# Late stage of an attention and GLU kernel: raw tokens in tiles of their own, output weights in the early ones' place, and a plan in which two DMA queues share one rate

## The chip, the cores and the metric

The kernel runs on one core of a Trainium2 chip. A core has five engines that run side by side, each through its own instruction list in order: TensorE (PE in the profile; PEld are its weight loads), VectorE (DVE), ScalarE (ACT), GpSimd (POOL) and SyncE (SP). SP and POOL also issue the transfers between the chip's memory (DRAM) and the core's SBUF; each has a queue of its own, and sixteen DMA engines move the data of both. TensorE writes to PSUM banks, from which VectorE and ScalarE read. The metric is the device time of one execution in microseconds, as the median of several runs; less is better.

## The reference

Attention over 32 heads (batch 4, heads 8, 768 tokens, 64 values each), in which a query sees only the keys whose six sign bits, taken from a projection, equal its own; then, on the joined heads (3072 tokens of 512 values), a gated layer with 1536 inner channels.

```python
q_bits = (np.einsum('bhsd,dk->bhsk', q, proj) > 0).astype(np.int64)    # keys alike
mask = q_bucket[:, :, :, None] == k_bucket[:, :, None, :]
scores = np.where(mask, scale * np.matmul(q, k.transpose(0, 1, 3, 2)), -1e9)
attn = softmax(scores)                                     # with 1e-9 added to the sum
x = np.matmul(attn, v).transpose(0, 2, 1, 3).reshape(B * S, H * D)
gate = 1.0 / (1.0 + np.exp(-(x @ w_gate)))
return (gate * (x @ w_val) @ w_out).astype(np.float32)
```

The weights of the layer arrive as 64-bit floats, which the kernel turns into 32-bit ones from their two integer halves.

## The kernel before

**A plan in the program.** The kernel doesn't emit its instructions in the order of its source. Each step is a task for one engine (or a choice of two) with a key, a duration in ns, the tasks it comes after, and the buffers (counted by name in `stock`, and in `late_stock` from the switch on) that it takes and gives. `Plan.order` (line 84) runs through time with these durations: each engine, when free, starts the ready task with the lowest key, and at the same key the one that was added first. The order that comes out is that of the instructions of each engine, and on the chip each engine then keeps it, whatever the real times are. A transfer (`dma`, line 312) takes its queue 600 ns and has a tail until its data count as landed: 2000 ns plus its bytes at 240 bytes per ns, behind the earlier transfers of the same queue. `wire` keeps this for the SP and the POOL queue apart, as if each had the whole rate (lines 156 to 161).

**Two stages.** Attention fills the first half of the span; its results go to DRAM as tokens `xd`. Beside it an early part of the gated layer runs (`moe_early`): for each batch and half, the first two blocks of 128 inner channels (J1 = 2), whose sums go to DRAM as `part`, by way of `ob` buffers of which there are two. Meanwhile the other weights are converted, combined and kept in DRAM, up to block 10. At `switch` (line 1206) the buffers of attention are given back and the late stage begins; the last early units still run into it.

**The late stage** (`products`, line 630) goes through the batches one by one. Each does its 768 tokens as two halves of 384 and the remaining inner channels in ten visits: jp from 1 to 5, and for each the gate and the value weights, streamed from DRAM by POOL's queue. A visit computes a 2 x 2 block product with seven products instead of eight (Strassen's scheme in Winograd's form). So it needs seven operands of the tokens: four blocks as they are and combinations of them. Before, they are made so: x0 = B11, x1 = B21, x3 = B22, x4 = B12 - B11, x5 = B22 - x4, x2 = B22 - B12, x6 = B21 - x5. Each is split into a high half, rounded (ScalarE, line 669), and a low half, the rest (VectorE, line 672); differences are VectorE's (line 664). In a visit the operands are used in the order x0, x1, x5, x4, x2, x6, x3 (the products m1, m2, m6, m5, m7, m4, m3, line 784), six matmuls each, and after the second, the fifth and the seventh TensorE does a piece of an output product (`y`, line 570). ScalarE copies interim sums to `t` tiles (t1, t16, t167, line 792), VectorE adds them to the other bank (line 799). From a gate visit come sigmoids (`sig`, line 856), in a value visit VectorE multiplies (lines 870 and 872) and the product is split into high and low again (lines 877 and 880).

**Tiles of the tokens.** x0, x2 and x3 use the tiles of the early part (`xr`, `xh`, `xl`), the other operands their own. The raw blocks B11 and B21 are loaded into the low halves of x0 and x1 themselves (line 652), which the low step then overwrites; B12 and B22 go into a tile `xb` (line 657). So the load of the next batch's B11 waits for the last visit's first product of this batch, and that of B21 for the second. Differences go to three tiles xt0 to xt2, that of x2 over B12.

**Late weights.** Blocks 10 and 11 (jp = 5) are loaded and converted in the first batch's visits (`load_w`, `load_pair`): first two output weights, then four chunks of gate and value weights, by way of one raw buffer. Steps of the conversion stand on lines 338 to 361, splits on 408, 411, 470 and 473, the store to DRAM on 476. Output weights 2 to 9 come back from DRAM (line 419).

**Ends of a batch.** The six pieces of the last output products run in the first visits of the next batch. Each is then added (`whole`, line 729) to the early part's sum, fetched from `part` into an `ob` buffer (line 743), and stored (line 746); fetches are chained one behind the other. The last batch uses the free token tiles instead.

Of the kernel before, what the change touches and what calls it, by code (L numbers as in the profile page):

```python
# [43 lines left out]
class Task:  # L44
# [7 lines left out]
    def __init__(self, key, options, after, take, give, tail, kind, behind=()):  # L52
# [11 lines left out]
        self.ready, self.size = 0, 0  # L64


class Plan:
# [16 lines left out]
    def order(self):  # L84
# [24 lines left out]
        while events:  # L109
# [10 lines left out]
            while again:  # L120
                again = False
                for e in SEEN:
# [60 lines left out]
def lsh_attention_glu_kernel(ctx, tc, q, k, v, proj, w_gate, w_val, w_out, out):  # L183
# [107 lines left out]
    def busy():  # L291
# [5 lines left out]
        ef=4, raw1=1, mid1=1, raw2=1, mid2=1, wk=1, xr=1, x=1, ob=2,  # L297
        t=0, zt=0, ws0=0, ws1=0, ws2=0, xb=0, xt0=0, xt1=0, xt2=0, x1=0, x4=0, x5=0, x6=0, wk2=0,
# [13 lines left out]
    def dma(key, nbytes, emit, engine="sp", **kw):  # L312
        t = add(key, engine, 600, emit, tail=LANDING + int(nbytes / RATE), **kw)
        t.size = nbytes
        return t
# [7 lines left out]
    def floats(key, load, after, last, name):  # L323
# [39 lines left out]
        a = dma(key, 524288, load_, after=after, take=[place])  # L363
# [11 lines left out]
    slots = dict(n=0, last=None)  # L375

    def load_w(key, n, j, early, last=None):
# [19 lines left out]
        def high():  # L397
            if early or last:
                if n == "o":
                    z["w"] = (later["w"] if last else w1).tile([P, 2, N_EL], F32R, name=f"w{n}{j}", tag=f"w{n}{j}")  # L400
# [15 lines left out]
        def fetch():  # L416
            w = later["w"].tile([P, 2, N_EL], F32R, name=f"w{n}{j}", tag=f"w{n}{j}")
# [3 lines left out]
        h = add(key, "act", 560, high, after=[e], take=[] if early or last else ["wk"])  # L421
# [73 lines left out]
    def load_x(u, b, g, stored):  # L495
# [19 lines left out]
        for c in range(KC):  # L515
            prev = add(
                FIRST, "act", 415, lambda c=c: high(c), after=[a, prev], take=["x"] if c == 0 else []
# [9 lines left out]
    def product(key, u, n, j, x, prev, last, pace=None):  # L527
# [14 lines left out]
        for c in range(KC):  # L542
            prev = add(
                key if c == 0 else OPEN, "pe", 3 * MM, lambda c=c: part(c), after=[prev, x["ready"][c], made[n, j], pace],
                take=z["bank"] if c == 0 else [], give=(["x"] + (["ws0"] if last == "end" else [])) if last and c == KC - 1 else [],
# [84 lines left out]
    def products(key, pair, prev, ends):  # L630
# [10 lines left out]
        TAG = dict(x0="xr", x2="xh", x3="xl")  # L641

        def slot(n):
            tag = TAG.get(n)
            X[n] = (xp if tag else later["w"]).tile(HALF_X, F32R, name=f"{n}_{b}", tag=tag or n)
            return f(X[n])

        raw = lambda n: f(X[n])[:, 1]

        def load_half(n, h):  # L650
            slot(n)
            nc.sync.dma_start(raw(n), xd_(h, 0))

        def load_second():
            X["b"] = later["w"].tile([P, 2, 2, GN], F32, name=f"xb_{b}", tag="xb")
            for h in range(2):
                nc.sync.dma_start(X["b"][:, h], xd_(h, 1))

        def difference(n, tag, first, second):
            if tag:  # L660
                X["r" + n] = later["w"].tile([P, 2, GN], F32, name=f"r{n}_{b}", tag=tag)
            else:
                X["r" + n] = X["b"][:, 0]
            nc.vector.tensor_sub(X["r" + n], first(), second())

        def high(n, of):
            if n not in X:
                slot(n)
            nc.scalar.copy(X[n][:, 0], of())

        def low(n, of, eng):
            eng.tensor_sub(X[n][:, 1], of(), f(X[n])[:, 0])

        here = lambda n: (lambda: raw(n))
        diff = lambda n: (lambda: X["r" + n])
        b12, b22 = (lambda: X["b"][:, 0]), (lambda: X["b"][:, 1])

        def lows(n, of, after, give=()):
            return add(
                FIRST, "dve", 900, lambda: low(n, of, nc.vector), after=after, give=give,  # L680
            )

        was = [a for g in range(NG) for a in stored[b, g]] + in_turn["x"]
# [580 lines left out]
```

## Time and profile before

| | |
|---|---|
| median of 3 runs | 1084.75 us (1080.46 to 1087.05) |
| profiled execution, its own time | 1079.3 us |
| its span, first to last instruction | 1077.5 us |
| mean granted clock of TensorE | 0.988 |
| TensorE busy, 553 to 600 us | 42.38 of 47.00 us |
| TensorE busy, 600 to 697 us | 91.10 of 97.00 us |
| TensorE busy, 697 to 818 us (one batch) | 117.09 of 121.00 us |
| TensorE busy, 818 to 937 us (one batch) | 115.46 of 119.00 us |
| TensorE busy, 937 us to the end | 129.79 of 140.50 us |

The profile is of one execution; its times run from the first instruction. The span is shorter than that execution's own time by 1.8 us, which lie before its first and after its last instruction. An engine's busy time counts its instructions; a wait is the idle time in front of one, put down to what ended last. The granted clock is the share of full speed that TensorE was given. "to landing" is the time from the issue of a transfer to its last data.

### The profile page before, as it was taken

What the parts mean: (1) busy time and instruction counts of PE and PEld (TensorE: products, weight loads), DVE (VectorE), ACT (ScalarE), POOL (GpSimd) and SP (SyncE); (2) the same over time, 40 slices, a digit from 0 to 9 for tenths busy, and PEclk for the clock granted to TensorE, in tenths of its full rate; (3) what the DMA queues carried; (4) which work ended last, traced back from release to release, by engine and by line L of the source; (5) the groups of instructions that cost most, each with busy time, mean ns of one, the idle gap of its engine ahead of it and who ended that gap; (6) DMA issues with size and microseconds to landing.
All of it is one profiled execution on the core that took longest, in us unless ns stands there. A gap on an engine that the chain in (4) does not pass through costs nothing.

```text
span 1077.5 us, 20497 instructions
## 1 busy us (share of the span) xinstructions
PE 1024.9 (95%) x8169; PEld 811.4 (75%) x8172; DVE 697.8 (65%) x1464; ACT 567.1 (53%) x1011; POOL 202.8 (19%) x230
## 2 busy tenths in 40 slices
PE   9999898999999999989999899999998999979998
PEld 5665566676675766656677789889997999879997
DVE  6898978889989778987746673464236333444333
ACT  2777776777786776857635433333234232422331
POOL 0013235344442423422031000000000000000000
PEclk9999998999999999999999999999999999989999
DMA  8345364764766456553168796466435743565521
GB/s 205 84 133 154 113 199 134 252 189 153 231 192 198 155 179 195 191 170 113 39 230 290 272 328 242 166 231 228 166 137 214 260 180 137 180 220 196 189 85 59
DMA packets 114561, 196.38 MB, mean 182 GB/s; under 512 B 61217, under 2 KB 83745, under 8 KB 109345
## 3 DMA queue, kind: packets, MB, share of 16 engines
q1 hardware_dynamic: 108544, 121.66, 36.0%
q0 software_dynamic: 5760, 73.40, 18.5%
q8 instruction: 64, 1.05, 0.4%
q14 instruction: 33, 0.26, 0.1%
q10 hardware_dynamic: 160, 0.00, 0.0%
HBM read 140.51 MB, written 41.94 MB: 169 GB/s over the span
## 4 chain that ended last, share of the span: by engine, by line
PE 77%; DVE 12%; DMA 6%; ACT 3%; issue 2%; POOL 1%; SPq 0%; ACTq 0%; DVEq 0%; POOLq 0%
PE y L570 13%; PE pv L1117 10%; PE sc L1034 8%; PE zBg L784 7%; PE zBv L784 7%; PE tp L1100 5%; PE zDg L784 4%; DVE e L1048 3%; PE zDv L784 3%; PE zo L570 3%; PE zg L537 3%; PE zv L537 3%; PE sc L1039 2%; PE zAg L784 2%; DMA x<-xd 2%
## 5 line engine op out<-in xcount | busy, mean ns | idle before, releaser
L1067 ACT ACTIVATE e<-e,st 128x768 f32<-128x768 f32 x192 | 196.5, 1026 | 71.6 <-DVE st L1060 71.5
L1048 DVE TENSOR_SCALAR_CACHE_REDUCE e<-sc 128x768 f32<-128x768 f32 x192 | 178.0, 951 | 21.8 <-PE sc L1039 21.2
L570 PE MATMUL y<-wo,gh 128*128 128x512 f32 x480 | 152.2, 399 | 0.0
L1117 PE MATMUL pv<-ef,vr 128*64 128x384 f32 x768 | 142.0, 499 | 0.0
L1100 PEld LDWEIGHTS tp<-ident,e 64*128 64x128 f32 x2304 | 85.5, 140 | 36.0 <-issue 20.2
L784 PE MATMUL zBv<-x,wsv 128*128 128x384 f32 x480 | 98.6, 340 | 9.9 <-ACT t167v L792 5.8
L570 PEld LDWEIGHTS y<-wo,gh 128*128 128x128 f32 x480 | 91.1, 190 | 15.7
L1100 PE MATMUL tp<-ident,e 64*128 64x64 f32 x2304 | 97.2, 227 | 5.3 <-ACT ef L1107 1.8
L784 PE MATMUL zBg<-x,wsg 128*128 128x384 f32 x480 | 97.3, 337 | 5.1 <-ACT t167g L792 3.7
L784 PEld LDWEIGHTS zBv<-x,wsv 128*128 128x128 f32 x480 | 86.5, 191 | 17.1 <-ACT t167v L792 7.4
L1107 ACT COPY ef<-tp 128x768 f32<-128x768 f32 x107 | 83.4, 792 | 25.5 <-PE tp L1100 25.2
L1034 PE MATMUL sc<-kh,ql 64*128 64x384 f32 x192 | 86.0, 448 | 9.2 <-DVE e L1048 2.9
L570 PE MATMUL y<-wo,gl 128*128 128x512 f32 x240 | 94.4, 393 | 0.0
L784 PEld LDWEIGHTS zBg<-x,wsg 128*128 128x128 f32 x480 | 85.7, 189 | 11.2 <-ACT t167g L792 4.4
L877 ACT CAST gh<-zt 128x384 fp32r<-128x384 f32 x80 | 41.0, 514 | 100.9 <-DVE zt L872 83.4
L1034 PE MATMUL sc<-kh,qsl 64*128 64x384 f32 x192 | 86.0, 448 | 7.1 <-DVE ef L1107 3.8
L1107 DVE COPY ef<-tp 128x768 f32<-128x768 f32 x85 | 80.4, 950 | 18.7 <-PE tp L1100 18.5
L1117 PEld LDWEIGHTS pv<-ef,vr 128*64 128x64 f32 x768 | 48.4, 137 | 52.5 <-issue 48.0
L1127 POOL TENSOR_TENSOR xs<-xs,rb 128x384 f32<-128x384 f32 x32 | 34.5, 1079 | 182.5 <-DVE xs L1124 117.6
L1039 PE MATMUL sc<-kb,qb 64*128 64x384 bf16 x384 | 65.2, 335 | 0.0
L1034 PE MATMUL sc<-kh,qsh 64*128 64x384 f32 x192 | 64.4, 335 | 0.0
L1034 PE MATMUL sc<-kl,qh 64*128 64x384 f32 x192 | 64.3, 335 | 0.0
(194 smaller groups left out, 2092.5 us busy)
## 6 DMA issues: line engine op xcount, KB each, us to landing
wsg<-kzg POOLq DMA_DIRECT2D x20, 1792.0 KB, 7.7
wsv<-kzv POOLq DMA_DIRECT2D x20, 1792.0 KB, 8.2
kzg<-wkg SPq DMA_DIRECT2D x10, 896.0 KB
kzv<-wkv SPq DMA_DIRECT2D x10, 896.0 KB
kr<-in_k_dram SPq DMA_DIRECT2D x64, 96.0 KB
qr<-in_q_dram SPq DMA_DIRECT2D x32, 192.0 KB
vr<-in_v_dram SPq DMA_DIRECT2D x16, 384.0 KB
qsh<-qh SPq DMA_DIRECT2D x32, 192.0 KB
```

What stands on the lines that cost most here:

```text
L537: nc.tensor.matmul(z["acc"][:, :GN], a[:, wc], x[xx][:, c, :], start=(c == 0 and i == 0), stop=(c == KC - 1 and i == 2),)
L570: nc.tensor.matmul(acc, a[:, slot, ts_], w, start=(first and i == 0), stop=(last and i == 2))
L784: nc.tensor.matmul(acc, streams[n, jp][:, c, wa, a_], X[x_][:, xa, c], start=first and c == 0 and i == 0, stop=c == 1 and i == 2, skip_gro ...
L877: nc.scalar.copy(side["h"][:, blk], w["z", blk])
L1034: nc.tensor.matmul(sc[:, j, :GN], q_[rows, c], z["k" + x][rows, h * GN : (h + 1) * GN], start=(m == 0), stop=False, tile_position=(j * D, 0),)
L1039: nc.tensor.matmul(sc[:, j, :GN], z["qb"][rows, c], z["kb"][rows, h], start=False, stop=True, tile_position=(j * D, 0),)
L1048: nc.vector.tensor_scalar(sp(e), gz["sc", t, h][:, :, :GN], -SCALE, None, op0=ALU.mult, op1=ALU.min, accum_out=gz["st", t][:, 0, h : h + 1],)
L1067: nc.scalar.activation(e, e, AF.Exp, bias=st[:, 2, h : h + 1], scale=st[:, 1, h : h + 1], accum_out=gz["su"][:, h * GT + t : h * GT + t + 1],)
L1100: nc.tensor.transpose(tp[:, r, at_ : at_ + D], gz["e", t, h][rows, c * P : (c + 1) * P], ident[rows, rows], tile_position=(r * D, 0),)
L1107: copy(gz["ef", c].rearrange("p (n r d) -> p r n d", r=2, d=D), gz["tp", c][:, :, :GN].rearrange("p r (n d) -> p r n d", d=D),)
L1117: nc.tensor.matmul(gz["pv"][rows, :GN], z["v"][:, h, c], gz["ef", c][:, h * GN : (h + 1) * GN], start=(c == 0), stop=(c == NC - 1), tile_p ...
L1127: nc.gpsimd.tensor_mul(gz["xs"], gz["xs"], gz["rb"])
```

## The change

- **Raw tokens.** B11 and B21 are loaded into tiles r0 and r1 of their own (in place of xt0 and xt1; r2 in place of xt2). The load no longer waits for the operands of the batch before, only for r0, r1 and xb. The combinations are formed in another order: T3 = B22 - B12 (over B12), T2 = T3 + B11 (in r2), T1 = B22 - T2 (over B11, after the low of x0), T4 = B21 - T2 (over B21, after the low of x1); x4 = T1, x5 = T2, x2 = T3, x6 = T4. Each operand is prepared when its own tile is given back, and these come back one by one: x2 and x3 are counted apart, and x2 is given after m7.
- **Late output weights** 10 and 11 take the tiles of the early ones 0 and 1 (`home`), after the last early products; they are loaded behind the gate and value weights instead of ahead of them.
- **Buffers.** Three `ob` instead of two, three `t` instead of two, two raw buffers for late weights instead of one.
- **The plan.** Two queues share the rate: where one has work on its wire, the other's transfer takes longer, and lengthens that. Loads of late weights and fetches of output sums count as landed 3000 ns later (`slack`). Token steps count 930 and 830 ns, where it was 900 and 800.

```diff
                     if t.tail:
                         free[e] = max(now, self.landings[0]) + ns
-                        self.wire[e] = max(self.wire[e], free[e]) + t.size / RATE
-                        t.tail = max(t.tail, self.wire[e] + LANDING - free[e])
+                        other = "sp" if e == "pool" else "pool"
+                        begin, alone = max(self.wire[e], free[e]), t.size / RATE
+                        both = max(0, self.wire[other] - begin)
+                        takes = alone + min(alone, both / 2)
+                        self.wire[e] = begin + takes
+                        self.wire[other] += min(both, takes) / 2
+                        t.tail = max(t.tail, self.wire[e] + LANDING + t.slack - free[e])
...
-        ef=4, raw1=1, mid1=1, raw2=1, mid2=1, wk=1, xr=1, x=1, ob=2,
+        ef=4, raw1=1, mid1=1, raw2=2, mid2=1, wk=1, xr=1, x2=1, x3=1, ob=3,
...
-    late_stock = dict(wk2=1, y=6, t=2, zt=3, xt0=1, xt1=1, xt2=1, ws1=1, ws2=1, xb=1, x1=1, x4=1, x5=1, x6=1)
+    late_stock = dict(wk2=1, y=6, t=3, zt=3, r0=1, r1=1, r2=1, ws1=1, ws2=1, xb=1, x1=1, x4=1, x5=1, x6=1)
...
-        a = dma(key, 524288, load_, after=after, take=[place])
+        a = dma(key, 524288, load_, slack=3000 if last else 0, after=after, take=[place])
...
+    def home(j):
+
+        early = j if j < J1 else j - NJ + J1 if j >= NJ - J1 else None
+        pool, tag = (later["w"], f"wo{j}") if early is None else (w1, f"wo{early}")
+        return pool.tile([P, 2, N_EL], F32R, name=f"wo{j}", tag=tag)
...
-        h = add(key, "act", 560, high, after=[e], take=[] if early or last else ["wk"])
+        h = add(key, "act", 560, high, after=[e] + (g_free if last else []), take=[] if early or last else ["wk"])
...
-        was = [a for g in range(NG) for a in stored[b, g]] + in_turn["x"]
-        l0 = dma(FIRST, 393216, lambda: load_half("x0", 0), after=was, take=["xr"])
+        was = [a for g in range(NG) for a in stored[b, g]]
+        l0 = dma(FIRST, 393216, lambda: load_first("B11", 0), after=was, take=["r0"])
         lb = dma(FIRST, 786432, load_second, after=was, take=["xb"])
-        l1 = dma(FIRST, 393216, lambda: load_half("x1", 1), after=was, take=["x1"])
+        l1 = dma(FIRST, 393216, lambda: load_first("B21", 1), after=was, take=["r1"])
...
+        def operand(n, of, after, give=()):
+            h = add(FIRST, "act", 830, lambda: high(n, of), after=after, take=["xr" if n == "x0" else n])
+            ready[n] = dve(lambda: low(n, of), [h], give=give)
...
-        h0 = highs("x0", here("x0"), [l0])
-        t1 = differences("x4", "xt0", b12, here("x0"), [l0, lb])
-        ready["x0"] = lows("x0", here("x0"), [h0, t1])
-        t2 = differences("x5", "xt1", b22, diff("x4"), [t1])
-        h4 = highs("x4", diff("x4"), [t1], ["x4"])
-        ready["x4"] = lows("x4", diff("x4"), [h4, t2], ["xt0"])
-        t4 = differences("x6", "xt2", here("x1"), diff("x5"), [t2, l1])
-        h1 = highs("x1", here("x1"), [l1])
-        ready["x1"] = lows("x1", here("x1"), [h1, t4])
...
+        d3 = dve(t3, [lb])
+        d2 = dve(t2, [d3, l0], take=["r2"])
+        operand("x0", "B11", [l0])
+        operand("x1", "B21", [l1])
+        operand("x5", "T2", [d2])
+        d1 = dve(t1, [d2, ready["x0"]])
+        operand("x4", "T1", [d1], ["r0"])
+        operand("x2", "T3", [d3])
+        d4 = dve(t4, [ready["x1"], d2], give=[])
+        operand("x6", "T4", [d4], ["r1"])
+        operand("x3", "B22", [lb])
+        add(FIRST, "sp", 0, lambda: None, after=[ready["x5"], d1, d4], give=["r2"])
+        add(FIRST, "sp", 0, lambda: None, after=[ready["x2"], ready["x3"], d1, d2], give=["xb"])
...
-                        FIRST, 262144, lambda: fetch(u, t, z), after=[parts[b, u, t]] + in_turn["ob"] + (list(ready.values()) if m is not None else []), take=take,
+                        FIRST, 262144, lambda: fetch(u, t, z), slack=3000, after=[parts[b, u, t]] + in_turn["ob"] + (list(ready.values()) if m is not None else []), take=take,
...
                     for late in range(JP2, JPN):
-                        for j in (2 * late, 2 * late + 1):
-                            load_w(1e3, "o", j, False, m1)
                         for w_ in "gv":
                             for c in range(2):
                                 load_pair(1e3, w_, late, c, m1)
+                        for j in (2 * late, 2 * late + 1):
+                            load_w(1e3, "o", j, False, m1)
...
-            prev = m7 = m(prev, "B", S3, "x2", False, False, [e16])
+            prev = m7 = m(prev, "B", S3, "x2", False, False, [e16], give=used("x2"))
...
-            prev = m3 = m(prev, "D", S4, "x3", False, True, [c22, *held], give=[slot_[1]] + used("x"))
+            prev = m3 = m(prev, "D", S4, "x3", False, True, [c22, *held], give=[slot_[1]] + used("x3"))
```

More of the change, by code (lines that the diff above doesn't have):

```diff
@@ L63, in __init__ @@
                 self.waits += 1
-        self.ready, self.size = 0, 0
+        self.ready, self.size, self.slack = 0, 0, 0
 class Plan:
@@ L310, in lsh_attention_glu_kernel, with dma @@
     CROWDED = 1600000
-    def dma(key, nbytes, emit, engine="sp", **kw):
+    def dma(key, nbytes, emit, engine="sp", slack=0, **kw):
         t = add(key, engine, 600, emit, tail=LANDING + int(nbytes / RATE), **kw)
-        t.size = nbytes
+        t.size, t.slack = nbytes, slack
         return t
@@ L399, in high @@
                 if n == "o":
-                    z["w"] = (later["w"] if last else w1).tile([P, 2, N_EL], F32R, name=f"w{n}{j}", tag=f"w{n}{j}")
+                    z["w"] = home(j)
                 else:
@@ L516, in load_x @@
             prev = add(
-                FIRST, "act", 415, lambda c=c: high(c), after=[a, prev], take=["x"] if c == 0 else []
+                FIRST, "act", 415, lambda c=c: high(c), after=[a, prev], take=["x2", "x3"] if c == 0 else []
             )
@@ L544, in product @@
                 key if c == 0 else OPEN, "pe", 3 * MM, lambda c=c: part(c), after=[prev, x["ready"][c], made[n, j], pace],
-                take=z["bank"] if c == 0 else [], give=(["x"] + (["ws0"] if last == "end" else [])) if last and c == KC - 1 else [],
+                take=z["bank"] if c == 0 else [], give=(["x2", "x3"] + (["ws0"] if last == "end" else [])) if last and c == KC - 1 else [],
             )
@@ L641, in products, with raw @@
         TAG = dict(x0="xr", x2="xh", x3="xl")
[L643 to L651, printed above, removed]
+        RAW = dict(B11="r0", B21="r1", T2="r2")
+        R = {}
+        def raw(n):
+            R[n] = later["w"].tile([P, 2, GN], F32, name=f"{n}_{b}", tag=RAW[n])
+            return R[n]
@@ L652, in load_half, with load_first @@
+        def load_first(n, h):
             nc.sync.dma_start(raw(n), xd_(h, 0))
         def load_second():
-            X["b"] = later["w"].tile([P, 2, 2, GN], F32, name=f"xb_{b}", tag="xb")
+            both = later["w"].tile([P, 2, 2, GN], F32, name=f"xb_{b}", tag="xb")
+            R["B12"], R["B22"] = both[:, 0], both[:, 1]
             for h in range(2):
[L657 to L664, printed above, removed]
@@ L666, in high @@
-        def high(n, of):
[L667 to L681, printed above, removed]
@@ L683, in products, with low @@
-        was = [a for g in range(NG) for a in stored[b, g]] + in_turn["x"]
-        l0 = dma(FIRST, 393216, lambda: load_half("x0", 0), after=was, take=["xr"])
+                nc.sync.dma_start(both[:, h], xd_(h, 1))
+        def high(n, of):
+            X[n] = (xp if n in TAG else later["w"]).tile(HALF_X, F32R, name=f"{n}_{b}", tag=TAG.get(n, n))
+            nc.scalar.copy(X[n][:, 0], R[of])
+        def low(n, of):
+            nc.vector.tensor_sub(X[n][:, 1], R[of], f(X[n])[:, 0])
+        was = [a for g in range(NG) for a in stored[b, g]]
@@ L685, in products @@
+        l0 = dma(FIRST, 393216, lambda: load_first("B11", 0), after=was, take=["r0"])
         lb = dma(FIRST, 786432, load_second, after=was, take=["xb"])
-        l1 = dma(FIRST, 393216, lambda: load_half("x1", 1), after=was, take=["x1"])
+        l1 = dma(FIRST, 393216, lambda: load_first("B21", 1), after=was, take=["r1"])
         ready = {}
-        def highs(n, of, after, take=()):
-            return add(FIRST, "act", 800, lambda: high(n, of), after=after, take=list(take))
-        def differences(n, tag, first, second, after):
-            return add(FIRST, "dve", 900, lambda: difference(n, tag, first, second), after=after, take=[tag] if tag else [])
```

33 lines of the change are left out of this document (18 added, 15 removed).

## The prediction

> **What bounds the kernel now.** I read the page first, then the waits of TensorE in the late stage, then granted clocks by window, then the timeline around each wait, then the chain of waits between them. The page (engine, busy us, share, instructions):
>
> ```profile
> span 1077.5 us, 20497 instructions
> ...
> PE 1024.9 (95%) x8169; PEld 811.4 (75%) x8172; DVE 697.8 (65%) x1464; ACT 567.1 (53%) x1011; POOL 202.8 (19%) x230
> ```
>
> TensorE is busy 95% of the span. The change leaves its instructions and, in the late stage, nearly all of their order as they are, since every product there is chained to the one before. So only TensorE's idle time there, and clock lost behind it, can go. The waits of TensorE from 580 us on (total us, times, longest):
>
> ```profile
> PE zAg L784 <- DVE x L672: 6.3, 3, 2.1
> PE zBv L784 <- ACT t167v L792: 5.8, 4, 1.9
> PE zBv L784 <- ACT t16v L792: 4.2, 1, 4.2
> PE zBg L784 <- ACT t167g L792: 3.7, 2, 3.0
> PE zBg L784 <- DVE zt L870: 1.4, 1, 1.4
> ```
>
> The first two rows are the three changes of batch (but for one wait in row two, below), the third is one wait near 960 us, the last two lie near 612 and 630 us. Windows (us; PE, PEld, DVE, ACT, POOL busy; granted clock; DMA share; GB/s) show that there is nothing between them (79.99 of 80 us busy) and that some waits also cost clock:
>
> ```profile
> 704.28:708.20 3.92, 3.92 (x12) 3.47 (x13) 3.88 (x5) 1.99 (x3) 0.00 (x0) 0.56 0.45 190
> ...
> 825.21:827.57 2.36, 2.36 (x11) 2.11 (x12) 2.36 (x3) 0.65 (x1) 0.00 (x0) 1.00 0.77 323
> ...
> 720.00:800.00 80.00, 79.99 (x420) 74.18 (x419) 29.88 (x56) 24.50 (x50) 3.69 (x7) 1.00 0.52 190
> ```
>
> **Part A: raw tokens in own tiles, summed ahead.** The first change of batch, in the timeline (start, us, engine, line, what; idle before and its releaser in brackets):
>
> ```profile
> 688.63 1.41 SPq L652 DMA_DIRECT2D x<-xd  x2
> 694.82 0.84 ACT L669 CAST x<-x 128x768 fp32r<-128x768 f32 x1 [2.23 <-DMA x<-xd]
> 694.82 0.96 DVE L664 TENSOR_TENSOR rx<-xb,x 128x768 f32<-128x768 f32 x1 [2.78 <-DMA x<-xd]
> 696.60 0.47 ACT L792 COPY t167v<-zBv 128x384 f32<-128x384 f32 x1
> 697.12 1.33 PE L784 MATMUL zBv<-x,wsv 128*128 128x384 f32 x6 [1.58 <-ACT t167v L792]
> 701.93 0.95 DVE L664 TENSOR_TENSOR rx<-x,rx 128x768 f32<-128x768 f32 x1
> 704.28 1.88 PE L784 MATMUL zAg<-x,wsg 128*128 128x384 f32 x5 [2.12 <-DVE x L672]
> ```
>
> The raw half of x0 can be loaded only when the last visit's first product has freed its tile (688.63). It lands at 694.8; ScalarE stands in order behind it with a token copy at its head, the copy t167v comes late, TensorE waits 1.58 us; then VectorE still has the differences before the low half of x1, and TensorE waits 2.12. Both name the load's landing as the start. After the change the four raw loads of a batch, 1.57 MB as before (first row below: size of one; second row: a weight stream and its us to landing),
>
> ```profile
> x<-xd SPq DMA_DIRECT2D x8, 384.0 KB
> ...
> wsg<-kzg POOLq DMA_DIRECT2D x20, 1792.0 KB, 7.7
> ```
>
> wait for r0, r1 and xb, which come free when the previous preparation ends, a whole batch earlier; T3 and T2 are made there and then, and the first order of business at the change is x0, then x1, in the order of use. The count stays: 4 differences and 7 lows on VectorE, 7 highs on ScalarE. What goes: 6.3 + 5.8 less the one wait of row two that is no change of batch,
>
> ```profile
> 598.39 1.32 PE L784 MATMUL zBv<-x,wsv 128*128 128x384 f32 x6 [0.62 <-ACT t167v L792]
> ```
>
> = 11.5 us, and the lost clock of the first change: the same stretch (five matmuls of zAg, two pieces of y and up to the next zBg) took 3.92 us there at 0.56 of the clock and 2.36 at the second change: 1.56. Together 13.0.
>
> The Trainium skill, "TensorE: Matmul & The Clock Gate", Part 1, says that the clock halves only after an idle window of about 3.4 us, which runs free of the kernel. The trace has a gap of 2.12 us with the clock lost and, at 825.21, one as long without. By that rule the 1.56 hangs on no gap of this length and may stay: the forecast would be 1065.4 where it is 1063.8 below.
>
> What comes in its place is VectorE's load. Back to back its steps take, and TensorE's groups take (chain of waits, start, us):
>
> ```profile
> 702.02 0.87 DVE rx L664
> 702.89 0.47 DVE gl L880
> ...
> 709.42 1.04 PE zDg L784 x6
> ...
> 711.50 1.39 PE y L570 x6
> ```
>
> A visit is 7 x 1.04 + 3 x 1.39 = 11.45 us. From the end of the last visit's second group (2.08) to the next visit's fifth, which needs the bank that the first sum frees (11.45 + 3 x 1.04 + 1.39 = 15.96), there are 13.9 us. In them VectorE has 3 sums, 4 gates and 4 lows of the gate at 0.47 (5.2), nine token steps at 0.87 (7.8), one more sum (0.47) and one output sum (0.7): 14.2, so 0.3 too much, and token steps of the new batch stand ahead of its sums, since they are numbered first at the same key. If the last two (1.74) and the output sum are ahead of it the wait is 2.4 us; if not, 0. I take 0.8 a change, nearer to the 0.3 of the count: 2.4. A third t tile loosens ScalarE's copies; I cost it at nothing. Part A: -10.6, between -13.0 and -5.8.
>
> **Part B: third output buffer and 3 us more in the plan for output fetches.** The wait near 960 us:
>
> ```profile
> 952.85 3.29 SPq L743 DMA_DIRECT2D ob_2l<-part  x2
> 954.03 0.53 POOL L1217 DMA_DIRECT2D wsv<-kzv  x1 [13.32 <-PE zDg L784]
> ...
> 962.71 0.69 DVE L729 TENSOR_TENSOR ob_2l<-y,ob_2l 128x512 f32<-128x512 f32 x1 [4.83 <-DMA ob_2l<-part]
> ...
> 964.84 2.29 PE L784 MATMUL zBv<-x,wsv 128*128 128x384 f32 x6 [4.15 <-ACT t16v L792]
> ...
> 971.06 1.23 PE L784 MATMUL zDv<-x,wsv 128*128 128x384 f32 x6
> ```
>
> The second 256 KB fetch leaves SP by 956.1 at the latest and lands at 962.7, 6.6 us on, beside a weight stream from the other queue. The plan reckoned 0.6 to issue, 2 and 262144/240 = 1.1 us, so it put the output sum 3 us too early in VectorE's order, and a gate, a high and t16v were caught behind it. With 3 us of slack, and up to 1.1 more for the shared rate, the sum is placed about where the data arrive; three fetches rather than two are ahead. What goes: 4.15, and clock: from 964.84 to 971.06 there are 6.22 us for groups of 1.04 + 1.39 + 1.04 = 3.47, so 2.75. Together 6.9. What is late next: the raw loads of the following batch now share SP's queue with these fetches at the first two changes. Between 0 (landing covered by the slack) and 6.9 (one such wait); I take 1.0, nearer the lower end because two buffers showed one such wait in three batches. Part B: -5.9.
>
> **Part C: late weights (two raw buffers, slack, shared rate, output weights last and in the early ones' tiles).** The first visits:
>
> ```profile
> 601.51 0.38 SPq L453 DMA_DIRECT2D rawg<-in_moe_w_gate_dram  x1
> ...
> 610.20 0.43 DVE L338 TENSOR_SCALAR exg<-rawg 128x512 int32<-128x512 int32 x1 [4.70 <-DMA rawg<-in_moe_w_gate_dram]
> ...
> 611.80 1.94 PE L784 MATMUL zBg<-x,wsg 128*128 128x384 f32 x6 [3.03 <-ACT t167g L792]
> ...
> 616.93 1.23 PE L784 MATMUL zBv<-x,wsv 128*128 128x384 f32 x6
> ...
> 617.28 0.32 SPq L476 DMA_DIRECT2D kzg<-wkg  x1
> ...
> 627.40 0.94 ACT L470 CAST wkg<-mfg 128x896 fp32r<-128x896 f32 x1 [3.11 <-DMA kzg<-wkg]
> ...
> 629.99 1.31 PE L784 MATMUL zBg<-x,wsg 128*128 128x384 f32 x6 [1.41 <-DVE zt L870]
> ```
>
> The raw load took 8.7 us where the plan had 2 + 2.2; now it has 7.2, and up to 2.2 more while POOL's queue moves. The store, by the landing times of this tile,
>
> ```profile
> DMA to landing us min/median/max: 8.3/9.0/9.7
> ```
>
> took 8.3 to 9.7 to free its buffer where the plan had 5.8, now up to 9.6. Two raw buffers let the next load run under the conversion. What goes: 3.03; its clock, 611.80 to 616.93 for 1.04 + 1.04 + 1.39, 1.66; and 1.41: 6.1. The conversions keep their count, so their steps still push the copies about: between 0 and all 6.1 stays; I take a quarter, 1.6, since every landing that TensorE waited for is now covered in the plan. Loading gate and value weights first has them in memory sooner; the output weights are needed only at the end of the first batch, some 100 us on, and their new tiles are free once the last early products are done, so I cost both at nothing; without that cover the first visits would gain a wait like the 3.03. Part C: -4.5.
>
> **Part D: the head of the late stage.** The first batch's raw loads no longer wait for the last early unit's tokens:
>
> ```profile
> 553.27 0.37 SPq L501 DMA_DIRECT2D xr<-xd  x1
> ...
> 562.49 0.44 PE L537 MATMUL zg<-xh,we 128*128 128x384 f32 x1 [0.65 <-ACT xh L508]
> ```
>
> They may let TensorE fill small waits such as this one, or run ahead of xr. The window
>
> ```profile
> 553.00:600.00 47.00, 42.38 (x216) 37.24 (x215) 25.16 (x35) 23.36 (x42) 9.07 (x10) 1.00 0.86 314
> ```
>
> has 47.00 - 42.38 = 4.6 us without TensorE and moves 314 GB/s, so 1.57 MB ahead of xr would be 5.0 us. Between -4.6 and +5.0; I take 0, since the early units come first at the same key.
>
> **Sum.** -10.6 - 5.9 - 4.5 + 0 = -21.0. The profiled execution took 1079.3 us (span 1077.5 and 1.8 around it): 1058.3. It lay 5.45 under the median of the three runs (1084.75), so on the median's footing 1063.8, said as 1064.
>
> **Rivals.** (1) VectorE takes back the changes of batch: the waits move from zAg to the group that needs the first sum's bank. For it: the 14.2 against 13.9; against: the token steps now have a whole visit before. Price 2.4 instead of 0.8 at three changes and the 1.56 of clock: +6.4, 1070. (2) DMA still lands later than planned, B and C stay: for it, DMA engines 0.86 busy from 553 to 600; against, the slack matches the measured 6.6 and 8.7. 1084.75 - 10.6 = 1074. (3) Slower: the raw loads stand in SP's queue ahead of transfers that TensorE will need sooner. Each such wait costs up to 6.9 with its clock (part B); three (head, first and second change) only eat the gain, and from five on, two at each change and one at the head, 34.5 - 21.0 = 13.5 makes 1098. For it: 1.57 MB is now issued next to the output fetches, beside a stream of 1.8 MB. Against: fetches of the previous batch are numbered before it. The Trainium skill, "DMA: Bandwidth & Descriptors", Issuing engines are not separate DMA queues, says that transfers of all queues interleave on the same 16 engines, so a load brought forward delays others; the 8.7 and 6.6 us above agree. (4) Nothing to see: the waits were caught elsewhere, 1080 to 1085.
>
> **How the numbers follow.** Forecast 0.56, rival one 0.18, two 0.14, three 0.07, four 0.05. A difference under about 1% (10.8 us) cannot be told from none here. Faster by more than that means below 1073.9: the forecast, all of one but a little (0.17) and less than half of two (0.05): 0.78. Slower is rival three, 0.07. The rest, 0.15, is within 1%. The range reaches down to all 26.0 gone with runs close to the profile (1053.3), and up over rival two: 1054 to 1076. The likeliest case alone spans 1056 to 1070.
>
> **What would show it.** Right: no SP wait for x0's tile before the raw loads; at a change of batch zBv and zAg wait under 1 us, and the granted clock stays 1.00 from 700 us on; output sums and conversions do not wait for DMA over 2 us. Wrong: a wait of zDg or zBg for a VectorE sum with token lows just ahead of it (rival one); a VectorE wait for ob or raw tiles with t16 or t167 behind it (rivals two and three); TensorE waits of over 3 us between 553 and 600. The whole falls if TensorE's late idle time stays above 20 us.

## The result, and the profile after

| | before | after |
|---|---|---|
| median | 1082.61 us (1078.39 to 1087.05, 4 runs) | 1053.32 us (1051.00 to 1056.21, 4 runs) |
| ratio of the times | | 0.973, 95% interval 0.968 to 0.978 |
| profiled execution | 1079.3 us | 1056.21 us, the longest of the four |
| span, mean clock | 1077.5 us, 0.988 | 1054.4 us, 0.995 |

The kernel is faster by 29.3 us at the median and by 23.1 between the two profiled executions. The forecast was 1064, with a range from 1054 to 1076: the direction was right and the gain too small, so that the time lies 0.7 below the range. The page of the changed kernel begins:

```profile
span 1054.4 us, 20508 instructions
...
PE 1017.8 (97%) x8172; PEld 807.4 (77%) x8172; DVE 699.9 (66%) x1464; ACT 566.2 (54%) x1011; POOL 203.6 (19%) x230
```

The operations of TensorE are the same; its busy time fell by 7.1 us, about what the lower clock had cost (0.988 and 0.995 of the two spans). The waits of TensorE from 555 us on (total us, times, longest; zg, zv and zo are products of the early units, zA, zB and zD the banks of the late visits):

```profile
PE zo L581 <- ACT sig L600: 2.0, 1, 2.0
PE zBv L789 <- ACT t167v L797: 0.9, 1, 0.9
PE zo L581 <- POOL gl L569: 0.9, 1, 0.9
PE zg L548 <- ACT xh L519: 0.6, 1, 0.6
PE zg L548 <- POOL xl L522: 0.6, 1, 0.6
PE zBg L789 <- ACT t167g L797: 0.6, 1, 0.6
PE zg L548 <- DVE xl L522: 0.4, 1, 0.4
```

All of them but the second lie before 600 us. From there on TensorE is busy without a break; the window's columns are us, then busy time of PE, PEld, DVE, ACT, POOL, the granted clock, DMA share and GB/s:

```profile
600.00:1040.00 440.00, 439.05 (x2300) 408.39 (x2299) 205.41 (x371) 157.29 (x302) 19.01 (x36) 1.00 0.57 208
```

Before, from 600 us to where the tail begins:

```profile
600.00:1063.00 463.00, 442.91 (x2275) 408.72 (x2274) 200.91 (x361) 155.44 (x297) 18.99 (x36) 0.99 0.54 195
```

The first change of batch in the timeline of the changed kernel, where before there were waits of 1.58 and 2.12:

```profile
688.30 1.57 ACT L671 CAST x<-B 128x768 fp32r<-128x768 f32 x2
689.45 0.95 DVE L674 TENSOR_TENSOR x<-B,x 128x768 fp32r<-128x768 f32 x1
...
696.21 4.91 SPq L661 DMA_DIRECT2D B<-xd  x2
...
699.15 1.20 PE L789 MATMUL zAg<-x,wsg 128*128 128x384 f32 x6
...
701.07 0.96 DVE L674 TENSOR_TENSOR x<-xb,x 128x768 fp32r<-128x768 f32 x1
701.58 1.21 PE L789 MATMUL zBg<-x,wsg 128*128 128x384 f32 x6
701.94 0.56 DVE L804 TENSOR_TENSOR sig<-zAg,t1g 128x384 f32<-128x384 f32 x1
...
702.63 1.24 PE L789 MATMUL zDg<-x,wsg 128*128 128x384 f32 x6
```

The raw blocks have long been there, so the highs of x0 and x1 run at 688.3, inside the last visit of the old batch, as soon as its first two products are done; the next raw loads leave at 696 for a batch that begins at 813. The last token low (701.07) still stands ahead of the sum that frees a bank (701.94), and TensorE takes that bank at 702.63, 1.05 after the group before, which is its ordinary pace.

For the rest it helps to cut each profile at three instructions: the issue of the last early unit's tokens (xr), the first and the last second group of a value visit (zAv). In the profile of before the latter two are

```profile
593.16 1.21 PE L784 MATMUL zAv<-x,wsv 128*128 128x384 f32 x6
...
1054.78 1.20 PE L784 MATMUL zAv<-x,wsv 128*128 128x384 f32 x6
```

and in that of the changed kernel

```profile
598.74 1.20 PE L789 MATMUL zAv<-x,wsv 128*128 128x384 f32 x6
...
1031.69 1.20 PE L789 MATMUL zAv<-x,wsv 128*128 128x384 f32 x6
```

"Head" is from xr to the first, "body" from the first to the last. Each visit with its three pieces takes 11.46 us when nothing waits, so the body also shows where time is lost. All kernels of the study, from one profile each:

| kernel | median us (runs) | xr issued | head | body | rest |
|---|---|---|---|---|---|
| before | see above | 553.3 | 39.9 | 461.6 | 22.7 |
| before_again | 1084.64 (1) | 556.6 | 39.9 | 463.7 | 22.8 |
| after | 1053.32 (4) | 556.5 | 42.2 | 433.0 | 22.7 |
| after_beside | 1051.87 (6) | 554.9 | 39.1 | 432.9 | 22.8 |
| tokens_alone | 1066.52 (4) | 556.3 | 48.9 | 436.5 | 22.7 |
| plan_alone | 1092.05 (4) | 555.8 | 44.5 | 470.3 | 22.7 |
| all_but_tokens | 1080.52 (10) | 554.2 | 40.6 | 459.0 | 22.8 |
| late_load | 1070.48 (10) | 555.2 | 39.7 | 450.4 | 22.8 |
| after_no_slack | 1054.43 (4) | 555.1 | 39.8 | 434.1 | 22.8 |
| own_rate | 1062.58 (4) | 555.4 | 48.5 | 435.8 | 22.7 |
| raw1 | 1067.17 (1) | 560.3 | 42.1 | 440.3 | 22.8 |
| after_head_slack | 1057.68 (4) | 555.2 | 44.5 | 433.0 | 22.7 |
| head_3 | 1050.84 (6) | 555.1 | 38.4 | 432.5 | 22.8 |
| head_4 | 1054.88 (6) | 556.0 | 40.0 | 433.6 | 22.8 |

The kernel before ran beside each group of four and had medians of 1080.45, 1080.61 and 1079.97 us there.

### The profile page after: what moved, and what is told of

Its sections match the earlier page's. It is cut to its first block, busy times and chain, and to the rows that moved or that the text cites. A ratio compares the mean times of both kernels' runs of the same rounds, so it can differ in the third digit from the quotient of the medians.

```text
span 1054.4 us, 20508 instructions
## 1 busy us (share of the span) xinstructions
PE 1017.8 (97%) x8172; PEld 807.4 (77%) x8172; DVE 699.9 (66%) x1464; ACT 566.2 (54%) x1011; POOL 203.6 (19%) x230
## 3 DMA queue, kind: packets, MB, share of 16 engines
q8 instruction: 64, 1.05, 0.4%
## 4 chain that ended last, share of the span: by engine, by line
PE 79%; DVE 11%; ACT 3%; issue 3%; DMA 3%; POOL 0%; SPq 0%; DVEq 0%; ACTq 0%; POOLq 0%
PE y L581 16%; PE pv L1122 10%; PE zBg L789 8%; PE zBv L789 8%; PE sc L1039 7%; PE tp L1105 5%; PE zDg L789 4%; PE zDv L789 4%; DVE e L1053 4%; PE zo L581 3%; PE sc L1044 2%; PE zg L548 2%; PE zAv L789 2%; PE zAg L789 2%; PE zv L548 2%
## 5 line engine op out<-in xcount | busy, mean ns | idle before, releaser
L1053 DVE TENSOR_SCALAR_CACHE_REDUCE e<-sc 128x768 f32<-128x768 f32 x192 | 178.2, 952 | 22.8 <-PE sc L1044 22.3
L789 PE MATMUL zBv<-x,wsv 128*128 128x384 f32 x480 | 96.4, 335 | 0.9 <-ACT t167v L797 0.9
L1039 PE MATMUL sc<-kl,qsh 64*128 64x384 f32 x192 | 64.6, 336 | 0.0
```

The source lines that it names most:

```text
L789: nc.tensor.matmul(acc, streams[n, jp][:, c, wa, a_], X[x_][:, xa, c], start=first and c == 0 and i == 0, stop=c == 1 and i == 2, skip_gro ...
L1039: nc.tensor.matmul(sc[:, j, :GN], q_[rows, c], z["k" + x][rows, h * GN : (h + 1) * GN], start=(m == 0), stop=False, tile_position=(j * D, 0),)
L1053: nc.vector.tensor_scalar(sp(e), gz["sc", t, h][:, :, :GN], -SCALE, None, op0=ALU.mult, op1=ALU.min, accum_out=gz["st", t][:, 0, h : h + 1],)
```

## The experiments

### One part alone, and all but that part

**tokens_alone** keeps the token part of the change and takes back the rest:

```diff
-                        other = "sp" if e == "pool" else "pool"
-                        begin, alone = max(self.wire[e], free[e]), t.size / RATE
-                        both = max(0, self.wire[other] - begin)
-                        takes = alone + min(alone, both / 2)
-                        self.wire[e] = begin + takes
-                        self.wire[other] += min(both, takes) / 2
+                        self.wire[e] = max(self.wire[e], free[e]) + t.size / RATE
...
-        ef=4, raw1=1, mid1=1, raw2=2, mid2=1, wk=1, xr=1, x2=1, x3=1, ob=3,
+        ef=4, raw1=1, mid1=1, raw2=1, mid2=1, wk=1, xr=1, x2=1, x3=1, ob=2,
...
-    late_stock = dict(wk2=1, y=6, t=3, zt=3, r0=1, r1=1, r2=1, ws1=1, ws2=1, xb=1, x1=1, x4=1, x5=1, x6=1)
+    late_stock = dict(wk2=1, y=6, t=2, zt=3, r0=1, r1=1, r2=1, ws1=1, ws2=1, xb=1, x1=1, x4=1, x5=1, x6=1)
...
-        early = j if j < J1 else j - NJ + J1 if j >= NJ - J1 else None
+        early = j if j < J1 else None
```

Beside these lines the slack is gone in both places, and the late output weights are loaded ahead of the gate and value streams again.

> Only the token part of the change (own raw tiles, sums in the new order, x2 and x3 given back apart); plan, slack, buffers and the place and order of the late output weights as before. Theory (each part takes away its own waits): the waits at the three changes of batch go. Counted from start to start of the second group of each visit they are 6.2, 4.7 and 4.6 us in the profile of before, 15.5 in all. The wait for an output fetch (7.1) and those for the late weights (6.6) stay, and the head of the late stage is some 2.4 us longer, as it is after the change. So 1082.6 - 15.5 + 2.4 = 1069.5, within 3. Rival (the token steps only move the waits to VectorE): changes of batch still lose over 2 us each and the time is over 1075.

Measured: 1066.52 us, ratio 0.988 (0.984 to 0.992). Counted from start to start as in the expectation, the changes of batch lose 3.7 us in all where it was 15.5, and the rival falls. That the time is still at the lower edge of what was expected is luck, since two errors largely cancel. TensorE's waits:

```profile
PE zo L576 <- DVE gf L559: 6.5, 1, 6.5
PE zo L576 <- POOL gl L564: 1.7, 1, 1.7
PE zDv L784 <- DVE zt L799: 1.3, 2, 0.8
PE zAv L784 <- DVE sig L799: 1.1, 2, 0.7
```

The body is within 3.5 us of the changed kernel's: the waits that parts B and C were to cure are gone too, without slack or buffers. The head is 9 us longer than before, where 2.4 were expected: the first difference waits for raw blocks that have not landed, with the last early unit's gate behind it on VectorE. That VectorE still waits long for output fetches here, but with nothing urgent behind it, shows in its own waits:

```profile
DVE ob_0l L729 <- DMA ob_0l<-part: 6.2, 3, 3.0
DVE ob_2l L729 <- DMA ob_2l<-part: 5.6, 2, 3.4
DVE ob_1l L729 <- DMA ob_1l<-part: 5.5, 2, 4.2
```

Those are 17.3 us of VectorE, more than before the change (12.4 for the same three tiles in its profile).

**plan_alone** is the kernel before with the shared rate and the slack, and nothing else:

```diff
+                        takes = alone + min(alone, both / 2)
...
+                        t.tail = max(t.tail, self.wire[e] + LANDING + t.slack - free[e])
...
-        a = dma(key, 524288, load_, after=after, take=[place])
+        a = dma(key, 524288, load_, slack=3000 if last else 0, after=after, take=[place])
```

> Only the plan of the change: shared rate of the two queues, 3 us of slack for late weights and output fetches; tiles, buffers and operations as before. Theory: the wait for an output fetch (7.1 us) and those for the late weights (6.6) go for the most part, the changes of batch keep theirs (15.5), since the raw load still starts at the last visit's first product. 1082.6 - 13.7 = 1069, within 4. Rival (the plan alone is what matters): with the landing planned later, the token copies no longer stand ahead of t167, the changes of batch lose under 3 us each and the time is under 1063.

Measured: 1092.05 us, ratio 1.012 (1.008 to 1.016), slower than before. Both theories fall:

```profile
PE zAg L789 <- DVE x L677: 16.0, 3, 5.4
PE zBv L789 <- DMA wsv<-kzv: 9.9, 1, 9.9
```

The waits of B and C are gone. But the token steps, which the plan now rightly sees arrive late, are put in a bunch behind the last visit's work, and one wait of 5.4 at each change replaces the 1.6 to 1.9 and 2.1 of before. And with one raw buffer and 3 us more for each of six loads in a row, the last value weights were issued at 673 where it was 635, so that a stream came 9.9 us late.

**all_but_tokens** has every part but the tokens, that is plan_alone with three output buffers, three t tiles, two raw buffers, and output weights last and in the early ones' place (`home`).

```diff
-        ef=4, raw1=1, mid1=1, raw2=1, mid2=1, wk=1, xr=1, x=1, ob=2,
+        ef=4, raw1=1, mid1=1, raw2=2, mid2=1, wk=1, xr=1, x=1, ob=3,
...
```

> Everything of the change except the token part: shared rate, slack, third output and t buffer, second raw buffer, late output weights last and in the early ones' tiles; raw tokens as before. The plan alone gave 1092: its changes of batch wait 16.0 us in all for token lows and one wait of 9.9 is for a weight stream whose late conversion came late. Theory (the second raw buffer and loading gate and value weights first exist to pay for the slack): the stream's wait goes, the changes of batch keep their 16 us and lost clock: 1078 to 1084. Rival (the slack spoils the late weights whatever the buffers): the stream's wait stays, 1088 or more. Second rival (buffers cure the changes of batch too): under 1070.

Measured: 1080.52 us, ratio 1.000 (0.997 to 1.003). The first theory holds: the stream's wait went, and

```profile
PE zAg L795 <- DVE x L683: 16.2, 3, 5.4
```

stayed. What the plan saves at B and C it gives back at the changes of batch, so it is worth nothing without the tokens.

### Taking the early load back

**late_load** is the changed kernel, with the raw loads made to wait for the first product of the batch before's last visit, as that of B11 did before the change:

```diff
-        was = [a for g in range(NG) for a in stored[b, g]]
+        was = [a for g in range(NG) for a in stored[b, g]] + last_first
...
+            if final:
+                last_first[:] = [m1]
```

> The changed kernel, but from the second batch on the raw loads wait for the first product of the last visit before, as the load of x0 did before the change; order of the sums, tiles, buffers and plan stay. Theory (loading ahead is what cures the changes of batch): the raw blocks land some 6 us into that visit, the token steps come in a bunch, TensorE loses 3 to 7 us at each of the three changes: 1053.5 plus 9 to 21, so 1062 to 1075. Rival (the new order of sums and the plan's knowledge of the queues are enough): under 1 us at each, 1053 to 1056.

Measured: 1070.48 us, ratio to before 0.990 (0.987 to 0.993), and 17 us above the changed kernel. The theory holds, the rival falls; the waits are back at the group that needs x1,

```profile
PE zAg L790 <- ACT x L672: 8.0, 3, 4.8
PE zAg L790 <- DVE x L675: 3.3, 3, 1.2
```

and the body is 17.4 longer (the changes lose 8.6, 4.8 and 4.8 us from start to start, the first more than the 7 expected). Loading ahead is what cures the changes of batch; the new order of sums and tiles given back one by one do not do it alone. Whether the early load would do it with the old order of sums was not run.

### Slack, rate and the second raw buffer, one out at a time

**after_no_slack** takes `slack=3000` away in both places.

```diff
-        a = dma(key, 524288, load_, slack=3000 if last else 0, after=after, take=[place])
+        a = dma(key, 524288, load_, after=after, take=[place])
```

> The changed kernel with slack 0. Theory (the slack carries parts B and C): VectorE waits for an output fetch or for raw weights again with a token or t copy caught behind it, and TensorE loses 3 to 13 us there: 1056 to 1066. Rival (third output buffer, second raw buffer and the shared rate do it without slack): no TensorE wait over 1 us after 600 us, and 1053 within 1.5.

Measured: 1054.43 us (1053.57 to 1054.95), beside 1051.0 to 1056.2 for the changed kernel. The rival holds: from 600 us on no wait of TensorE is over 0.7. The slack is not what carries B and C.

**own_rate** gives each queue the whole rate in the plan again and keeps the slack.

```diff
-                        other = "sp" if e == "pool" else "pool"
-                        begin, alone = max(self.wire[e], free[e]), t.size / RATE
-                        both = max(0, self.wire[other] - begin)
-                        takes = alone + min(alone, both / 2)
-                        self.wire[e] = begin + takes
-                        self.wire[other] += min(both, takes) / 2
+                        self.wire[e] = max(self.wire[e], free[e]) + t.size / RATE
```

> The changed kernel with the plan's wire as before the change, each queue at the whole rate; slack, tiles and buffers stay. With the token part alone TensorE waited 6.5 us near 574 for a gf of VectorE that stood behind a difference whose raw blocks had not landed; the changed kernel waits 2.0 there. Theory (the shared rate is what holds that wait down): 5 us or more of waiting at the head and its lost clock, 1058 to 1063. Rival (slack and buffers do it): under 3 us there, 1052 to 1056.

Measured: 1062.58 us, ratio to before 0.982 (0.978 to 0.987). As the theory says, the wait of tokens_alone is back, to the tenth:

```profile
PE zo L576 <- DVE gf L559: 6.5, 1, 6.5
```

The head is 9.3 longer than that of the changed kernel run beside it, the body 2.9. The shared rate pays mostly in the head, where both queues are full.

**raw1** has one raw buffer.

```diff
-        ef=4, raw1=1, mid1=1, raw2=2, mid2=1, wk=1, xr=1, x2=1, x3=1, ob=3,
+        ef=4, raw1=1, mid1=1, raw2=1, mid2=1, wk=1, xr=1, x2=1, x3=1, ob=3,
```

> The changed kernel with one raw buffer for the late weights. Theory: gate and value weights go first here, so their four loads, 9 to 12 us each with their conversion, end well before the tenth visit even one by one; no wait for a stream, 1052 to 1056. Rival (the second buffer is what keeps the stream in time): a TensorE wait of 3 us or more for wsv<-kzv near 680.

Measured: 1067.17 us in one run. Neither is right: no stream is late, but the output weights, now converted last, are:

```profile
PE y L581 <- ACT wo L419: 4.2, 1, 4.2
```

From that group to the next the visit took 7.1 us more than 11.46. Its attention stage was also 4 us longer than that of the others; up to there VectorE, ScalarE and GpSimd do the same steps in the same order, so this is not the edit's doing. So the second buffer pays for the output weights being last.

### The head, and the kernels once more

In the profile of the changed kernel the head had one new wait (timeline):

```profile
556.98 0.53 SPq L661 DMA_DIRECT2D B<-xd  x1
...
572.26 0.83 ACT L671 CAST x<-B 128x768 fp32r<-128x768 f32 x1 [2.80 <-DMA xb<-xd]
573.00 0.47 ACT L600 COPY sig<-zg 128x384 f32<-128x384 f32 x1
...
573.52 0.77 PE L581 MATMUL zo<-wo,gl 128*128 128x512 f32 x1 [1.97 <-ACT sig L600]
```

The first raw block, issued behind xr and beside two weight streams, was there only 15 us later, and a copy that TensorE needed stood behind its high. **after_head_slack**, **head_3** and **head_4** give these loads 6, 3 and 4 us of slack (here head_3):

```diff
-        l0 = dma(FIRST, 393216, lambda: load_first("B11", 0), after=was, take=["r0"])
+        l0 = dma(FIRST, 393216, lambda: load_first("B11", 0), slack=3000 if b == 0 else 0, after=was, take=["r0"])
```

and so for the other two loads.

> The changed kernel with 6 us of slack for the first batch's raw token loads. In the profile of the changed kernel TensorE waits 1.97 us at 573.5 for a copy of sig, behind a token copy whose raw block had not landed, and has 0.74 of its clock in the 6.5 us after. Theory: that is the head's loss; planned later, the copy of sig goes first, the wait and the lost clock (1.97 + 1.7) go, some of it comes back as small waits: 1050.5, within 1.5. Rival (the head is bound by the early units' own chain): the late stage begins no sooner, 1053.

> The changed kernel with 3 us of slack for the first batch's raw token loads. In its plan the copy of sig stands ahead of the first token high, where it stood behind, and TensorE's early pieces stay ahead of the first late product. Theory (that one copy is the head's new wait): the wait of 2.0 us near 574 and its lost clock go, 3 to 4 us less than the changed kernel run beside it. Rival (as with 6 us of slack, the token steps that come later hold up the last unit's gates): within 2 us of it or more.

> As head_3 with 4 us: one output copy more goes ahead of the first token high. Theory: as head_3, within 1 us of it. Rival: the gates of the last early unit wait, 1 to 4 us more than head_3.

> The changed kernel unchanged, beside these: 1053.3 within 2. The head from the issue of xr to the second visit's second group 42.2 us within 0.5; no wait over 1 us after 600 us, in contrast to the kernel before, whose waits differ from execution to execution.

Measured: 1057.68 with 6 us; then, beside each other, 1050.84 (1049.94 to 1051.72) with 3, 1054.88 with 4 and 1051.87 (1050.92 to 1053.86) for the changed kernel itself. Too much slack is worse: with 6 us a late product goes first, and the last unit's gates stand behind the token steps (4.6 us of waits for gl). With 4 the rival holds, 4.0 us more than with 3, part of it in the head and part in the body; which waits do it was not taken apart. With 3 the waits for sig are gone,

```profile
PE zo L581 <- POOL gl L569: 0.9, 1, 0.9
```

being the longest of its waits from 560 us on, and the median is 1.0 lower than that of the changed kernel, with runs that overlap; the expected 3 to 4 did not come, because in this execution of the changed kernel the wait it was to remove was short:

```profile
PE zo L581 <- ACT sig L600: 0.4, 1, 0.4
```

Its head took 39.1, not the 42.2 expected: the 2.0 us and the clock lost behind it belong to one execution. head_3, at 0.971 of before (0.968 to 0.975), has the lowest median of the study, though not by more than the runs spread.

**before_again** is the kernel before, unchanged, for a second profile.

> The kernel before, unchanged, for a second profile. Theory (its time varies by the clock that is lost behind its waits, which the changed kernel has not): the same waits of the same length at the same places, the granted clock differing at them; time within 1072 to 1090 and, at 1.00 of the clock after the waits near 612, 704 and 964, near 1072. Rival: waits of other lengths or at other places.

Measured: 1084.64 us, and the rival is nearer than the theory. The changes of batch wait as they did, but there is no wait near 960 us; a conversion waits for a store's landing near 656 instead, 3.35 us:

```profile
PE zBv L784 <- ACT t167v L792: 9.9, 5, 3.4
PE zAg L784 <- DVE x L672: 5.7, 3, 2.1
PE zBg L784 <- ACT t167g L792: 4.3, 2, 3.7
```

And the clock, which in the other execution was lost at the first of the three changes alone, is lost at all three:

```profile
714.41:717.82 3.41, 3.41 (x10) 2.93 (x10) 3.41 (x6) 1.99 (x3) 0.00 (x0) 0.50 0.08 34
827.05:830.46 3.41, 3.41 (x11) 3.41 (x12) 2.47 (x4) 1.94 (x3) 0.00 (x0) 0.50 0.00 0
949.93:953.34 3.41, 3.41 (x11) 3.12 (x11) 2.40 (x5) 0.93 (x3) 0.53 (x1) 0.50 0.00 0
```

From start to start the changes lose 6.4, 7.1 and 5.9 us here, where it was 6.2, 4.7 and 4.6.

## Why the prediction was right in direction and too small

Three steps of the sum failed, and with them the cause given for parts B and C: the price of the waits (26.0 us, measured 29.1), what was put back in their place (5.0, measured 0.4), and the step from the profiled execution to the median (5.45, some 4 of it chance). In part A the mechanism held.

**What can go.** Right: idle time of the late stage and clock behind it, nothing else. The body lost 28.7 us between the two profiled executions, the head of that execution gained 2.3, and its attention stage, which the change does not touch, was 3.2 longer; 28.7 - 2.3 - 3.2 is the 23.1 between the spans. In the run beside the others, with a head of 39.1, the span is 27.7 us shorter.

**The price of a wait.** The first error. The prediction added the idle time ahead of matmuls and, at three places, the lost clock: 26.0. From start to start of the same groups in the same profile it is more. Around the first change of batch:

```profile
688.44 1.20 PE L784 MATMUL zAv<-x,wsv 128*128 128x384 f32 x6
...
701.82 0.34 PE L784 MATMUL zAg<-x,wsg 128*128 128x384 f32 x1
...
717.25 1.20 PE L784 MATMUL zAv<-x,wsv 128*128 128x384 f32 x6
...
729.02 1.20 PE L784 MATMUL zAg<-x,wsg 128*128 128x384 f32 x6
```

These are 13.38, 15.43 and 11.77 us where a visit takes 11.46: 6.2 lost, while 1.58, 2.12 and 1.56 make 5.3. All the changes lost 15.5 where the prediction had 13.0, and the whole body 29.1 to 26.0. The idle time itself, 20.1 of the 26.0, was right; the missing 3.1 is time in which TensorE counts as busy, most of it at its restarts: the second change, where the clock stayed whole, lost 4.7 for waits of 1.71 and 2.11.

**What takes its place.** The second and larger error, of size: 2.4 for VectorE at the changes, 1.0 for output fetches and 1.6 for late weights, 5.0 in all. Measured: 0.2 at the three changes, nothing at the fetches, 0.2 in the first visits. The count for VectorE, 14.2 us of work for 13.9, was near the mark: from 688.98 to 702.50 it was busy without a break, 13.5 us, and its sum was done 0.13 before TensorE took the bank. The 0.7 between 14.2 and 13.5 is the output sum, which ran behind that sum (702.40) and not ahead of it. 5.0 - 0.4 and 3.1 are 7.7, and the predicted 21.0 with them is 28.7, what the body lost.

**Parts B and C.** The amounts went, the cause given was wrong. The prediction put them down to slack and buffers. Without slack the time is the same; with the token part alone both waits are gone too; and the wait at 960 us was one of those that a second execution of the same kernel does not have. In plan_alone both are gone as well, with the tokens as before. What moved them with the tokens alone, a different order of VectorE's steps or less on SP's queue at those times, was not taken apart. What the other parts do was tested: the shared rate holds the head (9 us), the second raw buffer lets the output weights be last. The third output buffer, the third t tile and the place of the late output weights were not taken out one at a time. That they gain nothing by themselves, in plan_alone and all_but_tokens, the prediction did not see; its sum took the parts for independent.

**Part D.** Taken as 0, with -4.6 to +5.0: +2.3 in the profiled execution, -0.8 in the next.

**The rivals.** VectorE taking back the changes, landings later than planned, raw loads in the way, nothing to see: none came. The third, transfers in each other's way, is seen in variants: a head of 48.5 to 48.9 us where the plan does not know of it.

**The footing.** The prediction added 5.45 us, since the profiled execution lay that far under the median of three runs, 1084.75. In the three later groups the kernel before has medians of 1079.97 to 1080.61, so some 4 of the 5.45 belonged to those three runs. That is the third error: of the 10.7 us by which 1064 missed, some 4 are this and the rest the size of the gain. The agreement of 29.3 at the median with 28.7 in the body is in part chance too: beside each other the medians differ by 28.1, the profiled spans by 23.1. And the best case that the prediction counted, all 26.0 gone from the profiled execution, is 1053.3, the very time measured; this is luck, since more went, from a slower start. The kernel before spreads from 1073 to 1088 us, with a mean clock between 0.996 and 0.985, the changed one from 1050.9 to 1056.2; that the waits which went made this spread fits the two profiles of before, but is not shown by them.

**The rule on the clock.** The Trainium skill's rule (TensorE: Matmul & The Clock Gate, Part 1: an idle window of about 3.4 us) would have left the 1.56 where it was. It went, with the waits of about 2 us beside it. How such waits cost clock in one execution and not in another can be read from the profiles of before, cut at the ends of the stretches at half clock, which last 3.41 us or twice that in the late stage. In the first profile they begin at 612.23, 704.39 and 963.81 us, 27 and 76 such lengths apart. There, around the waits for zAg at the first and the second change:

```profile
700.98:704.39 3.41, 1.29 (x8) 0.97 (x7) 3.41 (x7) 1.98 (x4) 0.00 (x0) 1.00 1.00 320
704.39:707.81 3.42, 3.42 (x10) 3.05 (x11) 3.42 (x5) 1.82 (x3) 0.00 (x0) 0.50 0.51 218
...
823.86:827.27 3.41, 2.06 (x10) 1.89 (x11) 3.41 (x5) 1.17 (x2) 0.00 (x0) 1.00 0.91 387
827.27:830.69 3.42, 3.42 (x21) 3.33 (x20) 3.29 (x5) 2.03 (x4) 0.00 (x0) 1.00 0.05 21
```

The first wait of 2.12 lay whole in one such stretch, TensorE was busy for 1.29 of its 3.41 us, and the next stretch ran at 0.50. The second, of 2.11, was shared by two stretches, and the clock stayed whole. In the second profile, at the first change:

```profile
704.17:707.58 3.41, 1.71 (x9) 1.60 (x10) 3.31 (x5) 2.94 (x5) 0.00 (x0) 1.00 0.02 5
707.58:711.00 3.42, 3.32 (x18) 2.74 (x16) 3.34 (x8) 1.71 (x4) 0.53 (x1) 1.00 0.38 88
711.00:714.41 3.41, 1.40 (x7) 1.36 (x8) 3.41 (x5) 1.13 (x2) 0.00 (x0) 1.00 0.98 416
```

After 1.71 busy us the clock stayed whole, after 1.40 came the half clock shown above. So these changes fit a window of 3.41 us that runs free of the kernel, but it need not be idle throughout: 2.0 us of idleness in it were enough, 1.7 were not.

## What to carry to other kernels

The stall between two batches was cured by a buffer that lets the load start a batch earlier; telling a static order of a later landing time, without that buffer, moved the wait and made it longer. Price a wait by the distance between the same two instructions with and without it, not by the idle time in front of one. And read two profiles of the kernel before, if it spreads, ahead of building on a single wait: the 4.2 us near 960 here were not in the second. Take the starting time, too, from more than three runs of such a kernel.

## What the runs showed of the hardware that had not been expected

- A 384 KB load that shared the engines with 3.6 MB of weight streams and stood behind a 768 KB load in its own queue was used 15.3 us after its issue (556.98 to 572.26); the step that used it had stood waiting for 2.8 us.
- Waits of about 2 us cost clock in some executions and not in others, of the same kernel at the same place: at the second and the third change of batch none in one profile, a stretch of 3.41 us at 0.50 in the next. It was lost where such a wait left TensorE 1.4 us or less busy in a stretch of 3.41 us, and not where the wait fell across the border of two.
